# Linear attention and a gated feed-forward on one core: gates of two more token chunks by seven products, elementwise work moved to GpSimd, and a new order of steps

## The chip, the core and the metric

The kernel runs on one core of a Trainium2 chip. A core has TensorE (PE, with its weight loads shown as PEld), VectorE (DVE), ScalarE (ACT), GpSimd (POOL) and SyncE (SP). Each engine works through its own queue in order and waits there on semaphores, and DMAs are issued from the queues of SP, POOL and ACT. The metric is device time in microseconds (us): the time before is the median of three runs.

## What is computed

```python
def phi(x): return where(x > 0, x, exp(x) - 1) + 1          # = min(exp(x), max(x, 0) + 1)
q_p, k_p = phi(q), phi(k)                                    # q, k, v: 8 batches, 8 heads, 576 rows, 64
kv  = einsum('bhsd,bhse->bhde', k_p, v);  z = sum(k_p, axis=2)
num = einsum('bhsd,bhde->bhse', q_p, kv)
x   = num / (einsum('bhsd,bhd->bhs', q_p, z)[..., None] + 1e-6)   # as 4608 rows of 512
out = ((x @ w1) * (x @ w2)) @ w3 @ w_out                     # w1, w2: 512x1024, w3: 1024x1024, w_out: 1024x512
```

All inputs and the output are f32 in memory. On the chip the products take bf16 and add up in f32.

## The kernel before

The 4608 rows are cut into nine chunks of 512. Chunks 0 to 7 hold the first 512 rows of a batch each, and chunk 8 the last 64 rows of all eight. w3 and w_out are first multiplied to one matrix, `wf_sb` (1024x512), so that a chunk needs its gate, (x w1)(x w2), a tile `ab` of 1024x512 in bf16, and then one product with `wf_sb`.

The whole program is one list of steps, the string `ORDER`, from which `step` calls one small function for each word. The list fixes the order on every engine: each engine does its own instructions in the order in which the steps stand. A trailing "+" chooses the second engine for the elementwise part of a step (for a load: the POOL queue instead of SP's). The letters that matter here, with batch or chunk b:

- `Lb.g`, `Mb.g`, `Nb.g`: loads of half a batch of k, q, v (512 KB) into a tile of the pool `ld`, which has 13 buffers. `Rb.0`, `Rb.1`: the last 64 rows of q and k, and of v.
- `xb.g` and `Xb.g` (k and q): `phi_exp`, exp on ACT. `yb.g`, `Yb.g`: `phi_max1`, max(x, 0) + 1, of f32 to bf16. `zb.g`, `Zb.g`: `phi_min`, the minimum of the two, bf16. A half of 128x1024 is done in two instructions of 128x512. g = 2 stands for the last rows, of q and k together.
- `vb.g`: v to bf16. `Kb`: `kv_full`, the 18 matmuls of kv and z of a batch and the copy out of PSUM. `Tb.0`: a DMA transpose of phi(q).
- `Ab.j`: `nat`, four matmuls for 128 rows of num and den, then three DVE instructions (add 1e-6, reciprocal, product) that write x (`xn`). `Db.0`: a DMA transpose of the chunk's x into `xt`, on SP's queue; `Db.1` for the last rows.
- `Fb.f`: `f_unit`, one of eight gate tiles of a chunk with eight matmuls: four give x w1 (`a_ps`), four x w2 (`b_ps`), each of 128x512; ACT copies the one to SBUF, DVE multiplies it with the other.
- `Gb.q.i`: `g_unit`, product i (1 to 7) of quarter q. Four quarters of seven products (Winograd's form of Strassen's scheme) give a chunk's gate: each product is four matmuls of 128x256 with weights out of w1, w2 or their sums (`ws_make`, steps `e`), and with columns of x or of their differences (`xs_make`, steps `db.i`). Products 1, 3 and 4 are copied to SBUF by ACT, products 2, 5 and 6 are added to such a copy by DVE, product 7 is copied in half by ACT and multiplied by DVE.
- `mb.q.i`: `g_mul`, the f32 product (128x256) that makes a block of `ab` from the sums of products 2, 5 and 6.
- `Ob.m`: `o_unit`, eight matmuls of 128x512 with `wf_sb` and a copy. `S`, `H`, `Q`: stores of the output.

Before the change, chunks 0 to 5 take the eight tiles of `F`, and chunks 6, 8 and 7 (in this order) the 28 products of `G`. The sums of weights and of x, and the ring of twelve f32 tiles for `G`, are laid into buffers of `ld` that no load needs any more (`from_ld`); `f_close` has a ring of four f32 tiles of its own. All `e`, `d`, `m` and `y` steps run on DVE. PSUM has four buffers for `mm` (`a_ps`, `b_ps` and the products `t`, `t2`), and three single ones, of which `ou0`/`ou1` hold `u` of the products or the sums of `O`.

Of the kernel before, what the change touches and what calls it, by code (L numbers as in the profile page):

```python
# [20 lines left out]
def kernel(  # L21
# [177 lines left out]
    def phi_min(name, b, g):
# [7 lines left out]
        e, y = (t.rearrange("p (c u j d) -> p c u j d", c=2, u=2, d=D) for t in (e, y))  # L207
        for c in range(2):
            nc.vector.tensor_tensor(out=p[0][:, 2 * g + c].rearrange("p j u d -> p u j d"),  # L209
                                    in0=e[:, c], in1=y[:, c], op=ALU.min)  # L210
# [519 lines left out]
```

## Time and profile before

| | |
|---|---|
| median of three runs | 250.21 us (249.04 to 250.46) |
| the profiled execution | 249.9 us, of which 248.0 us are the span from its first to its last instruction |
| granted TensorE clock, mean | 0.991 |
| ACT busy | 131.9 us (53%) |
| DMA | 49.43 MB, 199 GB/s over the span |

A "line" such as L422 is a line of the program. A group of the profile reads: line, engine, operation, out<-in, shape, xcount | busy us, mean ns of one | idle time before it and what ended it. A window reads: its length, then busy us and number of instructions for PE, PEld, DVE, ACT and POOL, the granted clock, the busy share of the DMA engines (which may pass 1, as packets of several queues overlap), and GB/s. A piece of the chain of waits reads: its start, its length, what ran. The releasers are inferred from semaphores.

### The profile page before, as it was taken

The page shows a single profiled execution, that of the slowest core. Times are in us where ns is not written, and L with a number is a line of the kernel's source. Part 1 is how long each engine was busy: PE and PEld are TensorE (multiplying, and loading weights), DVE is VectorE, ACT ScalarE, POOL GpSimd, SP SyncE. Part 2 cuts the span into 40 slices and gives each one's busy share as a digit, 9 for nine tenths or more (in the row PEclk, how much of TensorE's full clock was granted, in tenths as well). Part 3 has the DMA queues.
Part 4 walks back from the last instruction along what each step waited for, and adds up shares of the span by engine and source line. Part 5 has one row for each costly group of instructions (what it writes and reads, how often), then busy time and mean ns, then how long its engine had stood idle before and what let it go on. Part 6 is the DMA issues. An engine that isn't in the chain of part 4 may idle for free.

```text
span 248.0 us, 4281 instructions
## 1 busy us (share of the span) xinstructions
PE 230.9 (93%) x1548; PEld 133.6 (54%) x1548; DVE 187.4 (76%) x434; ACT 131.9 (53%) x213; POOL 49.4 (20%) x79
## 2 busy tenths in 40 slices
PE   0699868999999999999999999999999999999994
PEld 0445455654454554345445544545488688578542
DVE  3227769777898847788768799988899999779810
ACT  2206667658756725675563383536466377245321
POOL 8546368665014050500000000000000000000000
PEclk9999988999999999999999999999999999999999
DMA  7999999999999999999999999917750133040144
GB/s 159 193 202 310 295 211 211 194 259 288 287 219 329 236 234 273 217 304 282 288 362 268 284 270 221 295 37 174 169 193 0 22 65 107 3 169 1 44 152 145
DMA packets 64021, 49.43 MB, mean 199 GB/s; under 512 B 32480, under 2 KB 58848, under 8 KB 64000
## 3 DMA queue, kind: packets, MB, share of 16 engines
q1 hardware_dynamic: 52928, 36.31, 58.3%
q0 software_dynamic: 10928, 12.72, 25.2%
q8 instruction: 12, 0.20, 0.3%
q10 hardware_dynamic: 144, 0.13, 0.2%
q14 instruction: 9, 0.07, 0.1%
HBM read 38.80 MB, written 9.44 MB: 194 GB/s over the span
## 4 chain that ended last, share of the span: by engine, by line
PE 67%; DMA 21%; ACT 3%; DVE 3%; SPq 2%; issue 2%; POOL 0%; ACTq 0%; DVEq 0%; POOLq 0%
PE o_ps L536 21%; PE a_ps L362 12%; PE b_ps L362 12%; DMA q<-in_q_dram 10%; PE gu L422 9%; DMA w3b<-in_moe_w_dram 7%; PE gt L422 6%; DMA k<-in_k_dram 4%; PE nd L310 3%; PE kvp L245 2%; SPq L104 1%; ACT e L179 1%; PE o_ps L561 1%; PE kvp L249 1%; DVE qj L209 1%
## 5 line engine op out<-in xcount | busy, mean ns | idle before, releaser
L536 PE MATMUL o_ps<-wf_sb,ab 128*128 128x512 bf16 x280 | 64.2, 379 | 0.0
L362 PEld LDWEIGHTS <-w_sb 128*128 128x128 bf16 x384 | 36.5, 98 | 40.6 <-issue 0.8
L362 PE MATMUL a_ps<-xt,w_sb 128*128 128x512 bf16 x192 | 50.3, 379 | 0.5 <-ACT a_sb L367 0.5
L362 PE MATMUL b_ps<-xt,w_sb 128*128 128x512 bf16 x192 | 50.3, 379 | 0.0
L536 PEld LDWEIGHTS <-ab 128*128 128x128 bf16 x280 | 26.8, 98 | 29.3
L368 DVE TENSOR_TENSOR ab<-a_sb,b_ps 128x512 bf16<-128x512 f32 x48 | 32.5, 683 | 11.5 <-PE b_ps L362 5.9
L538 ACT COPY o_sb<-o_ps 128x512 f32<-128x512 f32 x30 | 17.4, 585 | 42.8 <-PE o_ps L536 28.8
L367 ACT COPY a_sb<-a_ps 128x512 f32<-128x512 f32 x48 | 27.7, 585 | 22.2 <-PE a_ps L362 21.8
L326 DVE TENSOR_TENSOR xn<-nd,r 128x512 bf16<-128x512 f32 x30 | 20.7, 691 | 1.0
L422 PEld LDWEIGHTS <-spare 128*128 128x128 bf16 x192 | 18.7, 98 | 2.2
L179 ACT ACTIVATE e<-q 128x1024 bf16<-128x1024 f32 x16 | 16.8, 1057 | 5.7 <-DMA q<-in_q_dram 5.0
L310 PE MATMUL nd<-kv,qt 128*128 128x130 bf16 (+1 forms) x160 | 16.6, 228 | 2.9 <-ACT kv L254 1.8
L179 ACT ACTIVATE e<-k 128x1024 bf16<-128x1024 f32 x16 | 16.8, 1056 | 3.2 <-DMA k<-in_k_dram 3.1
L310 PEld LDWEIGHTS <-qt 128*128 128x128 bf16 (+1 forms) x160 | 11.8, 103 | 12.2 <-issue 3.5
L454 DVE TENSOR_TENSOR spare<-spare,gt 128x512 f32<-128x512 f32 x24 | 16.1, 680 | 1.8 <-PE gt L422 0.9
L154 PE MATMUL wf_ps<-wt_sb,w3t 128*128 128x512 bf16 x64 | 16.5, 403 | 0.6 <-DMA wt_sb<-in_moe_w_out_dram 0.6
L450 ACT COPY spare<-gu 128x512 f32<-128x512 f32 x24 | 13.6, 587 | 3.9 <-PE gu L422 3.7
L422 PEld LDWEIGHTS <-w_sb 128*128 128x128 bf16 x144 | 14.0, 98 | 2.7 <-issue 0.3
L465 DVE TENSOR_TENSOR ab<-spare 128x256 bf16<-128x256 f32 x36 | 14.1, 417 | 0.1
L114 POOL DMA_DIRECT2D qk32r<-in_q_dram x14 | 9.0, 644 | 23.3 <-ACT a_sb L367 10.7
L209 DVE TENSOR_TENSOR qj<-e,y 128x512 bf16<-128x512 bf16 x32 | 12.1, 418 | 2.0 <-ACT e L179 1.8
L422 PE MATMUL gu<-spare 128*128 128x256 bf16 x96 | 13.4, 272 | 0.0
(87 smaller groups left out, 294.0 us busy)
## 6 DMA issues: line engine op xcount, KB each, us to landing
out_dram<-o_sb SPq DMA_DIRECT2D x15, 512.0 KB, 3.9
q<-in_q_dram SPq DMA_DIRECT2D x13, 512.0 KB, 8.1
k<-in_k_dram SPq DMA_DIRECT2D x12, 512.0 KB, 7.0
v<-in_v_dram SPq DMA_DIRECT2D x12, 512.0 KB, 9.0
w3b<-in_moe_w_dram POOLq DMA_DIRECT2D x8, 256.0 KB, 10.0
...
```

What stands on the lines that cost most here:

```text
L154: nc.tensor.matmul(wfs[i], w3ts[i][:, kc, :], wo_sb[:, kc, :], start=(kc == 0), stop=(kc == FC - 1))
L179: nc.scalar.activation(out=e, in_=x, func=AF.Exp)
L209: nc.vector.tensor_tensor(out=p[0][:, 2 * g + c].rearrange("p j u d -> p u j d"), in0=e[:, c], in1=y[:, c], op=ALU.min)
L310: nc.tensor.matmul(nds[g][rows, i * 2 * E1:(i + 1) * 2 * E1], w, kvs[b % 2][:, i, g].rearrange("p u e -> p (u e)"), start=True, stop=True)
L326: nc.vector.tensor_tensor(out=dst.rearrange("p (g h) e -> p g h e", g=2), in0=v4[:, :, :, 0:D], in1=r[rows].unsqueeze(3).to_broadcast([n, ...
L362: nc.tensor.matmul(ps, w[:, kc, f * P:(f + 1) * P], xt_of(c)[:, :, kc, :], start=(kc == 0), stop=(kc == KC - 1))
L367: nc.scalar.copy(out=a_sb, in_=a_ps)
L368: nc.vector.tensor_mul(out=abs_[c][:, f, :], in0=a_sb, in1=b_ps)
L422: nc.tensor.matmul(t[:, w], l, r, start=(first and w == 0 and k == 0), stop=(k == 1), skip_group_check=True)
L454: nc.vector.tensor_tensor(out=s, in0=o, in1=t, op=ALU.add)
L536: nc.tensor.matmul(o_ps, ab[:, f, m * P:(m + 1) * P], wf_sb[:, f, :], start=(f == 0), stop=(f == FC - 1))
L538: copy_of(alt)(out=rows_of(c, m // 2)[:, m % 2], in_=o_ps)
```

## The change

- Chunks 4 and 5 are also done by seven products. Now 56 products of `G` and 24 `m` steps take the place of 16 `F` steps, and eight `d` steps come with them.
- The sums of weights go into `wo_sb` (w_out's own tile, free after `wf_sb` is made, and no longer shared with another) and the new `wx_sb`; the differences of x go into a pool of two tiles `xs`. The f32 tiles of `G` and `F` share one ring of eight. The pool `ld` shrinks from 13 buffers to 8.
- A half's minimum of phi is one instruction of 128x1024 rather than two of 128x512, for which phi(k), phi(q) and the transposed phi(q) are laid out by j and then c.
- On GpSimd now: all eight `e` steps, eight of the 32 maxima of a half and one of the last rows, 11 of the 20 `d` steps and 43 of the 60 `m` steps. Eight `O` copies rather than five are on DVE.
- From the step behind `L4.0` on, the list of steps is in a new order. The part before that is unchanged. Functions that no step called are removed.

```diff
-    ld = ctx.enter_context(tc.tile_pool(name="ld", bufs=13))
+    ld = ctx.enter_context(tc.tile_pool(name="ld", bufs=8))
...
-    wt_sb = wpool.tile([P, 4, FC // 2, HN], BF16)
-    wo_sb = wt_sb.rearrange("p i (a c) n -> p (i a) (c n)", c=2)
+    wo_sb = wpool.tile([P, FC, DM], BF16)
+    wx_sb = wpool.tile([P, 4, 2, NQ * P], BF16)
...
-            p[0] = t[:, 0:JW].rearrange("p (c j u d) -> p c j u d", j=NJ, u=2, d=D)
+            p[0] = t[:, 0:JW].rearrange("p (j c u d) -> p c j u d", j=NJ, u=2, d=D)
+            p[2] = t[:, 0:JW].rearrange("p (j h d) -> p h j d", j=NJ, d=D)
...
-        e, y = (t.rearrange("p (c u j d) -> p c u j d", c=2, u=2, d=D) for t in (e, y))
-        for c in range(2):
-            nc.vector.tensor_tensor(out=p[0][:, 2 * g + c].rearrange("p j u d -> p u j d"),
-                                    in0=e[:, c], in1=y[:, c], op=ALU.min)
+        e, y = (t.rearrange("p (h j d) -> p h j d", j=NJ, d=D) for t in (e, y))
+        nc.vector.tensor_tensor(out=p[2][:, 4 * g:4 * g + 4], in0=e, in1=y, op=ALU.min)
...
-            qts[b, 0] = t[:, 0:NB].rearrange("p (c j) t -> p c (j t)", j=NJ)
+            qts[b, 0] = t[:, 0:NB].rearrange("p (j c) t -> p j c t", j=NJ)
...
-        a_sb = sm.tile([P, NCH], F32, tag="f", name="a_sb", bufs=4)
+        a_sb = fsm("a_sb").rearrange("p a n -> p (a n)")
...
-        s[i] = from_ld(("w", w, i // 2), [P, 2, 2, NQ * P], BF16)[:, i % 2]
+        s[i] = wx_sb[:, i] if w else wo_sb.rearrange("p (i k) n -> p i k n", k=2)[:, i]
...
-            xss[c] = from_ld(("x", c), [P, 4, 2, 2, P], BF16)
+            xss[c] = xt_p.tile([P, 4, 2, 2, P], BF16, tag="xs", name="xs", bufs=2)
...
     def fsm(name):
-        if not spare.get("ring"):
-            spare["ring"] = True
-            for n in range(6):
-                t = from_ld(("f", n), [P, 2, 2, HN], F32)
-                ring.extend((t[:, 0], t[:, 1]))
-        return ring.pop(0)
+        return sm.tile([P, 2, HN], F32, tag="f", name=name, bufs=8)
...
-    v3.1 S0.1 A2.1 y3.1 R5.1+ z3.0 z3.1 v3.0 v3.2 O1.1+ O1.0 T3.0 D2.0 S0.0 L4.0 K3 R4.1+ R4.0+ O1.3
-    A3.0 O1.2 A3.2 L4.1 v4.2+ F2.6 A3.3 F2.3 N4.1 y4.0 F2.1 M4.0 x4.0 A3.1 x4.1 F2.0 M4.1 y4.2 v5.2+
...
-    G7.3.2 G7.1.2 G7.3.7 m7.3.2 m7.3.6 m7.1.2 O8.2 m7.3.5 O8.3 m7.0.5 O7.0 m7.2.6 O7.1 H8.2 m7.2.5
-    H8.3 O8.0 m7.1.6 S7.0 O8.1+ S8.0 O7.2 H7.2 Q7.3
+    v3.1 S0.1 A2.1 y3.1 R5.1+ z3.0 z3.1 v3.0 v3.2 O1.1+ O1.0 T3.0 D2.0 S0.0 L4.0 R4.0+ L4.1 x5.2
+    M4.0 y4.2 x4.2 M4.1 R4.1+ R6.0+ z5.2 y4.0+ K3+ N4.0 O1.2 v5.2+ A3.0 z4.2 v4.2+ F2.6 A2.4 F2.7
+    M5.1 N4.1 F2.0 y6.2 A3.3 x4.1 x4.0 z4.0 M5.0 F2.2 y4.1+ F2.4 M6.0 e1.0+ S1.0 z4.1 X4.0 v4.0+
+    Y4.0 X4.1 X5.1 O1.3 A3.2 Y4.1+ e1.2+ Z4.1 Y5.1 R7.0+ v4.1 F2.3 F2.1 K4 F2.5 e0.2+ S1.1 A3.1 Z5.1
+    x6.2 R6.1+ X5.0 O2.0+ X6.0 Z4.0 O2.3 Y5.0 Z5.0 L5.0 x5.0 O2.2 x7.2 Y6.0 y5.0 D3.0 v6.2 A3.4 T4.0
+    z5.0 O2.1 L5.1 F3.0 F3.7 Z6.0 y7.2+ e1.1+ A4.2 x5.1 z6.2 F3.5 M6.1 M7.0 y5.1 F3.2 A4.0 X6.1 z5.1
+    F3.3 N5.1 N5.0 L6.0 X7.0 N6.0 L6.1 e0.0+ S2.0 v5.0+ v5.1 F3.1 Y6.1+ x6.0 A4.1 S2.1 F3.6 F3.4
+    y6.0+ T5.0 A4.3 Z6.1 O3.3+ x6.1 v6.0 K5 O3.2 O3.1 y6.1 z6.0 D4.0 D1.1 e1.3+ z6.1 Y7.0 N6.1 Z7.0
+    z7.2 N7.1 A5.3 e0.1+ O3.0 e0.3+ d4.0 d4.2 d4.1+ A5.2 G4.1.1 G4.1.2 G4.0.1 L7.1 G4.0.4 A5.0
+    m4.1.2+ v6.1+ G4.1.3 G4.1.4 G4.0.3 G4.1.5 G4.0.6 d4.3+ G4.2.4 G4.0.5 G4.1.7 v7.1 G4.0.2 A5.1
+    R7.1+ m4.1.5+ m4.0.6+ L7.0 G4.0.7 G4.3.1 G4.3.4 m4.0.5+ y7.1+ G4.3.2 S3.0 x7.0 G4.3.3 G4.1.6
+    G4.2.1 m4.1.6+ A4.4 D5.0 m4.0.2+ G4.2.2 G4.3.5 G4.3.6 G4.2.3 d5.0 m4.3.2+ T6.0 K6 G4.2.5 G4.3.7
+    v7.2 G5.3.4 m4.2.2+ M7.1 m4.3.6+ A5.4 G4.2.7 y7.0+ G5.0.4 G4.2.6 x7.1 G5.1.4 A6.3 O4.1 S3.1 d5.2
+    m4.3.5+ z7.1 X7.1 m4.2.5+ m4.2.6+ N7.0 d5.1+ z7.0 A6.0 O4.2+ Y7.1+ D3.1 Z7.1 O4.3 T7.0 A6.4
+    G5.0.1 G5.1.1 G5.1.2 G5.0.3 v7.0 d5.3+ A6.2 G5.1.3 S4.1 G5.0.6 G5.0.5 m5.1.2+ G5.0.2 K7 G5.1.5
+    G5.0.7 G5.1.6 A6.1 m5.0.2+ m5.0.6+ G5.1.7 O4.0 m5.1.5+ D6.0 m5.0.5+ A7.4 G5.3.1 G5.3.2 G5.2.1
+    m5.1.6+ m5.3.2 G5.2.2 m5.2.2+ G5.3.3 G5.3.6 G5.2.4 d6.0 m5.3.6+ G5.2.3 G5.3.5 d6.1+ G5.2.6
+    G6.0.4 G5.2.5 G5.3.7 m5.2.6+ A7.2 G6.1.4 G5.2.7 m5.3.5+ d6.3 d6.2+ G6.1.1 G6.3.4 G6.1.2 G6.1.3
+    D5.1 D7.1 A7.0 G6.0.1 G6.1.5 S4.0 m5.2.5+ m6.1.2+ G6.1.6 G6.0.3 G6.0.6 m6.1.6+ G6.1.7 G6.0.5
+    m6.0.5+ A7.1 d8.0 d8.1+ G6.0.2 O5.1 d8.3+ G6.0.7 m6.0.2 G6.2.4 G6.3.1 m6.1.5 A7.3 D7.0 m6.0.6+
+    O5.0 G6.3.3 G6.3.6 G6.2.1 G6.3.2 G6.3.5 G6.2.3 d8.2+ m6.3.2+ G8.1.4 G6.2.6 G6.2.5 G6.3.7 m6.3.6+
+    S5.0 m6.2.6 G6.2.2 m6.3.5 G8.0.4 G6.2.7 O5.3 m6.2.2+ m6.2.5+ O5.2 G8.1.1 d7.0 d7.2 G8.1.2 G8.0.1
+    m8.1.2+ G8.0.2 G8.1.3 d7.1+ G8.0.3 m8.0.2 d7.3+ G8.1.6 G7.1.4 G8.0.5 G8.1.5 m8.0.5 G8.2.4
+    m8.1.6+ G8.0.7 G8.3.4 G8.1.7 G8.0.6 m8.1.5+ m8.0.6 O6.2 G8.3.1 G8.3.2 G8.2.1 G8.3.3 m8.3.2 S5.1
+    G8.3.6 G8.2.3 G8.3.5 G8.2.2 G8.2.5 G8.3.7 G8.2.6 G7.0.4 m8.2.5 G8.2.7 m8.2.2+ m8.3.6+ m8.3.5
+    O6.3+ m8.2.6+ O6.0+ O6.1 G7.0.1 G7.0.2 G7.1.1 G7.0.3 S6.1 G7.0.6 G7.1.3 S6.0 G7.0.5 G7.2.4
+    m7.0.5 G7.1.5 G7.0.7 G7.1.6 G7.1.2 m7.1.6+ G7.1.7 O8.2+ O8.3 G7.2.1 m7.1.5 G7.2.2 m7.0.2+ G7.3.1
+    m7.1.2 G7.2.3 G7.3.2 G7.3.3 G7.2.5 m7.2.2+ G7.3.4 m7.2.5 G7.3.5 G7.2.7 G7.2.6 G7.3.6 G7.3.7 H8.3
+    O8.0+ H8.2 m7.3.5+ O8.1 m7.3.2+ O7.0 S8.0 m7.2.6 O7.1 m7.3.6 m7.0.6+ O7.2 S7.0 H7.2 Q7.3
```

107 lines of the change are left out of this document (9 added, 98 removed).

## The prediction

> **What bounds the kernel now.** I read the page's busy times and slices first, then the chain of waits, then three stretches of the span.
>
> ```profile
> span 248.0 us, 4281 instructions
> PE 230.9 (93%) x1548; PEld 133.6 (54%) x1548; DVE 187.4 (76%) x434; ACT 131.9 (53%) x213; POOL 49.4 (20%) x79
> PE   0699868999999999999999999999999999999994
> DVE  3227769777898847788768799988899999779810
> PE 67%; DMA 21%; ACT 3%; DVE 3%; SPq 2%; issue 2%; POOL 0%; ACTq 0%; DVEq 0%; POOLq 0%
> PE o_ps L536 21%; PE a_ps L362 12%; PE b_ps L362 12%; DMA q<-in_q_dram 10%; PE gu L422 9%; DMA w3b<-in_moe_w_dram 7%; PE gt L422 6%; DMA k<-in_k_dram 4%; PE nd L310 3%; PE kvp L245 2%; SPq L104 1%; ACT e L179 1%; PE o_ps L561 1%; PE kvp L249 1%; DVE qj L209 1%
> 50.00:174.00 124.00, 122.80 (x721) 61.12 (x720) 101.80 (x234) 71.58 (x110) 19.05 (x31) 1.00 1.04 256
> 174.00:236.00 62.00, 61.99 (x481) 45.16 (x480) 54.74 (x125) 32.47 (x63) 0.00 (x0) 1.00 0.27 78
> ```
>
> TensorE is busy without a break from about 50 us to 236 us. Busy can mean waiting, so I compared the pace of the two ways to make a gate with each other, in pieces of the chain:
>
> ```profile
> 64.68 0.86 PE a_ps L362 x4
> 65.54 0.86 PE b_ps L362 x4
> 186.42 0.87 PE gt L422 x8
> 187.30 0.87 PE gu L422 x8
> ...
> L422 PEld LDWEIGHTS <-spare 128*128 128x128 bf16 x192 | 18.7, 98 | 2.2
> ```
>
> Four matmuls of 512 columns take 0.86 us, and eight of 256 take 0.87 us: in both cases the time goes with the columns, and the extra weight loads of the products, 98 ns each at a pace of 109, are hidden. So TensorE is the bound, and only fewer columns or fewer of the remaining gaps shorten the run. VectorE is second: 54.74 of 62 us in the last stretch, where the products run, and GpSimd did nothing there at all. That is why the products were not free to spread: they need more elementwise work.
>
> **What TensorE saves.** An F step is 0.86 + 0.86 = 1.72 us; 16 of them are 27.5 us. A product is half of 0.87, and 56 of them are 24.4 us. The difference is **-3.2 us**, if nothing else comes to bound.
>
> **What VectorE and ScalarE pay.**
>
> ```profile
> L368 DVE TENSOR_TENSOR ab<-a_sb,b_ps 128x512 bf16<-128x512 f32 x48 | 32.5, 683 | 11.5 <-PE b_ps L362 5.9 <-ACT a_sb L367 5.1 <-PE tpr L277 0.2
> L454 DVE TENSOR_TENSOR spare<-spare,gt 128x512 f32<-128x512 f32 x24 | 16.1, 680 | 1.8 <-PE gt L422 0.9 <-ACT spare L450 0.7
> L459 DVE TENSOR_TENSOR ab<-spare,gu 128x256 bf16<-128x256 f32 x12 | 4.9, 416 | 0.6 <-ACT spare L458 0.6
> L465 DVE TENSOR_TENSOR ab<-spare 128x256 bf16<-128x256 f32 x36 | 14.1, 417 | 0.1
> L209 DVE TENSOR_TENSOR qj<-e,y 128x512 bf16<-128x512 bf16 x32 | 12.1, 418 | 2.0 <-ACT e L179 1.8
> L184 DVE TENSOR_SCALAR y<-k 128x1024 bf16<-128x1024 f32 x16 | 11.1, 692 | 2.7 <-DMA k<-in_k_dram 2.7
> L396 DVE TENSOR_TENSOR spare<-w_sb 128x1024 bf16<-128x1024 bf16 x4 | 2.7, 685 | 0.0
> L407 DVE TENSOR_TENSOR spare<-xt 128x512 bf16<-128x512 bf16 x4 | 1.7, 419 | 0.6 <-DMA xt<-xn 0.6
> L538 DVE COPY o_sb<-o_ps 128x512 f32<-128x512 f32 x5 | 3.4, 687 | 8.4 <-PE o_ps L536 8.3
> L367 ACT COPY a_sb<-a_ps 128x512 f32<-128x512 f32 x48 | 27.7, 585 | 22.2 <-PE a_ps L362 21.8
> L450 ACT COPY spare<-gu 128x512 f32<-128x512 f32 x24 | 13.6, 587 | 3.9 <-PE gu L422 3.7
> L458 ACT COPY spare<-gu 128x256 f32<-128x256 f32 x12 | 4.5, 373 | 4.9 <-PE gu L422 4.2 <-DVE ab L459 0.5
> ```
>
> VectorE: 16 gate products go (-10.9), 24 sums of 0.680 and 8 products of 0.416 come (+19.6). It does 17 `m` steps rather than 36 (-7.9), 9 `d` steps rather than 12 (-1.3), no `e` step (8 x 0.685, -5.5), and eight maxima fewer (-5.5). A minimum of 128x1024 in one piece should cost what the bf16 instruction of that size at L396 does, 0.685 rather than 2 x 0.418: 32 times -0.15 are -4.8. Three copies of `o_ps` more are +2.1. Sum: about -14 of 187 us. ScalarE: -16 x 0.585, + 24 x 0.587 + 8 x 0.373, - 3 x 0.585: +6, to some 138 us. Both stay far under TensorE over the whole.
>
> **What GpSimd pays.** No row shows an elementwise product on it, so its price is bounded by what it has done:
>
> ```profile
> L714 POOL MEMSET const-float32-0.0<- 128x1 f32 x1 | 0.1, 98 | 0.2 <-issue 0.2
> masks.py:197 POOL MEMSET ident<- 128x128 bf16 x1 | 0.3, 272 | 0.0
> masks.py:199 POOL TENSOR_SCALAR_AFFINE_SELECT ident<-ident 128x128 bf16<-128x128 bf16 x1 | 0.3, 287 | 0.1
> L114 POOL DMA_DIRECT2D v32r<-in_v_dram x14 | 8.7, 627 | 14.0 <-DVE vr L221 10.7 <-DMA v32r<-in_v_dram 1.3 <-DMA qk32r<-in_k_dram 1.1
> ```
>
> From 1 to 128 elements the memset grows by 1.37 ns an element; one input (287) adds nearly nothing. I take 98 ns + 1.37 ns an element with one input and twice the slope with two: an `m` step 0.80, a `d` step 1.50, an `e` step 2.90, a maximum of a half 1.50. The low end is VectorE's own rows (0.417, 0.42, 0.685, 0.69). The high end is 287 ns for 128 elements without a fixed part, doubled for two inputs: 1.15, 2.30, 4.60, 2.30.
>
> The densest stretch of the new order runs from `O3.2` (just behind `K5`) to `G6.1.7`. It holds 68 products, 7 `O`, 14 `A` and 2 `K` on TensorE, and on GpSimd 25 `m`, 6 `d`, 3 `e`, 3 maxima and two loads of v's last rows.
>
> ```profile
> L310 PE MATMUL nd<-kv,qt 128*128 128x130 bf16 (+1 forms) x160 | 16.6, 228 | 2.9 <-ACT kv L254 1.8
> L245 PE MATMUL kvp<-vt,kj 128*128 128x130 bf16 x96 | 7.1, 219 | 0.0
> L249 PE MATMUL kvp<-vr,qj 128*128 128x260 bf16 x16 | 4.4, 273 | 0.0
> L324 DVE TENSOR_SCALAR r<-nd 128x8 f32<-128x8 f32 x30 | 4.8, 160 | 6.2 <-PE nd L310 6.0
> L325 DVE RECIPROCAL r<-r 128x8 f32<-128x8 f32 x30 | 6.1, 203 | 1.1
> L326 DVE TENSOR_TENSOR xn<-nd,r 128x512 bf16<-128x512 f32 x30 | 20.7, 691 | 1.0
> ```
>
> TensorE: 68 x 0.435 + 7 x 1.72 + 14 x 0.42 (16.6 / 40) + 2 x 1.73 (7.1 / 6 + 4.4 / 8) = 51 us. VectorE: 28 sums, 9 gate products, 14 times 1.05 for `A`, 6 minima, 2 maxima, 6 `d`, and three smaller steps make about 47. GpSimd: 25 x 0.80 + 6 x 1.50 + 3 x 2.90 + 3 x 1.50 + 2 x 0.63 = 43.5 us; 18 at the low end, 64.5 at the high one. At my price it fits behind TensorE's 51 with a sixth to spare, so I charge nothing for it; at the high end it would be late by 13.
>
> The Trainium skill, in the GPSIMD Engine Reference, section 3.1 (Elementwise), puts a two-input operation at about 2.6 cycles of 1.2 GHz an element, and in section 4.1 (Engine selection) advises against GpSimd for elementwise products as it is about twice as slow as VectorE. By that an `m` step is an estimated 0.55 us and the stretch some 31, which would leave the sum as it is; no row here shows it.
>
> **New waits, +1.1 us.** First, `D5.0` now stands close in front of its use. From `A5.1`, its last input, to `G5.3.4`, the first product that reads a difference of chunk 5, TensorE has 13 products, one `A` of half the rows and `K6`, 5.7 + 0.2 + 1.7 = 7.6 us. Against it stand 1.05 us for `A` on VectorE, 0.42 for `d5.0`, and the transpose:
>
> ```profile
> DMA to landing us min/median/max: 2.5/4.8/8.9
> ```
>
> (the DMA transposes of L351). With the median that is 6.3 us and fits, with the longest 10.4 and is 2.8 late; VectorE waits at `d5.0` with the sum of `G4.2.5` and the half-product of `G4.3.7` behind it, and TensorE stops when their banks are not emptied. I charge 0.5 (0 to 2.8). Second, `Z7.1` stands two short VectorE steps behind its maximum `Y7.1`, which queues on GpSimd behind three `m` and `d5.1`: 0.2 (0 to 1). Third, VectorE and GpSimd may slow each other down (below): 0.4 (0 up to the rival's price).
>
> **A small gain at the start, -0.3 us.** The order there is the same, but the chain holds 1% of `qj` minima (2.5 us), which get 18% shorter: 0 to -0.45. The other edits cost nothing by themselves: with eight load buffers rather than 13 a load waits for the eighth before it, which by the order has long been read (`L7.1` is the tightest, about ten us of TensorE ahead of its use); the ring of eight f32 tiles leaves at the least one product's time, 0.44 us, between the release of a tile and the next writer. That cover is thin: a late `m` on GpSimd would show as ScalarE waiting, then TensorE.
>
> **Sum:** 249.9 (span 248.0 + 1.9 around it) - 3.2 - 0.3 + 1.1 = 247.5 for an execution like the profiled one, which lies 0.3 under the median; so 247.8 against 250.2, 1% faster.
>
> **Rivals.** (A) *GpSimd becomes the bound of the dense stretch.* It takes in-order work there that everything waits for: `d` steps before products, `m` steps that give back f32 tiles and, at the end of a chunk, hold up `O`. It decides from 1.18 times my price (51 / 43.5). At 1.35 times it is 58.7, 7.5 late; 249.9 + 7.5 - 3.2 = 254; at the high end, 260. For it: no spare tile, and a price without a row. Against: the memsets. The same end is reached by contention: VectorE's instructions with two inputs in SBUF, or copies from it at double rate, take in that stretch 6 minima, 6 `d`, 1 `m` and 2 maxima, about 8.5 us; if they doubled while GpSimd works, VectorE would need 55.5 rather than 47, 4.5 over TensorE: 251. The Trainium skill says in the GPSIMD Engine Reference, sections 1 (Specifications) and 8 (Key points), that GpSimd shares its SBUF interfaces with VectorE and contends with just such instructions; no run so far shows it.
>
> (B) *The loads bind.* Counted in TensorE's time of the steps in front, the new order wants the first half of q of batch 6 some 20 us earlier and that of batch 7 some 30 us earlier on ScalarE's queue, which also empties PSUM, and the DMA engines are at 1.04 of their time from 50 to 174 us. Each load that lands late stops both. Against it: their tiles are free ten us or more ahead. Two late landings of 1.5 us each would cost what was saved: 250.
>
> (C) *The sum is right and the waits don't come*, since VectorE is relieved: 249.9 - 3.2 - 0.5 = 246.2.
>
> (D) *The products don't save.* If the weight loads were late behind other traffic, 56 products could take the 27.5 us of what they replace: 250. The pace of 0.87 speaks against it.
>
> **How the numbers follow.** My forecast 0.50, A 0.26, B 0.10, C 0.12, D 0.02. A measurement tells about 0.5%, 1.25 us, from no change. C and nine tenths of the forecast lie under 248.96: faster 0.57. D, half of B and what is left of the forecast are within: 0.13 with a little of A; A for the most part and half of B make slower 0.30. The range goes from just under C, 245.8, to A at 1.35 times, 254; the forecast's own is 246 to 249.
>
> **What would show it.** Right: 224 more matmuls of 128x256 at 0.435 a product; minima of 128x1024 near 0.685; GpSimd under 90 us busy behind the loads; VectorE near 173 us; no new gap of TensorE over half a us from `G4` on but at `d5.0`. Wrong: `m` steps over 0.94 us on GpSimd, VectorE's two-input instructions longer than before, ScalarE waiting on GpSimd for its f32 tile, or on a load of q.

## The result, and the profile after

| | before | after |
|---|---|---|
| median | 249.62 us (248.40 to 250.46, 4 runs) | 273.13 us (271.21 to 273.99, 4 runs) |
| ratio to before, 95% interval | | 1.0935 (1.0857 to 1.1013) |
| span of the profiled execution | 248.0 us | 269.2 us |

The kernel became 9% slower; the prediction had been 1% faster, with a range that ended at 254 us. The page of the changed kernel answers to the one shown of before as follows (busy times and share of the span, the slices, the chain that ended last).

```profile
span 269.2 us, 4565 instructions
PE 236.9 (88%) x1644; PEld 143.8 (53%) x1644; DVE 198.0 (74%) x377; ACT 138.6 (51%) x231; POOL 144.5 (54%) x150
...
PE   0699969999999995698989499986989999999994
...
DVE  3237897778888768999879959859888867747720
...
POOL 8445596573202399991549359993484727202310
...
PE 29%; POOL 7%; DVE 3%; DMA 2%; ACT 1%; issue 0%; POOLq 0%; DVEq 0%
```

Three things are to be seen. TensorE has lost its unbroken row of nines between the 16th and the 30th slice (about 101 to 202 us). GpSimd's own nines stand in the same part, from the 15th to the 27th slice, but for one in the 6th. And VectorE, which was to lose 14 us of work, has gained 11 (187.4 to 198.0) with 57 instructions fewer. The groups, with different shapes kept apart, say which instructions grew:

```profile
L440 POOL TENSOR_TENSOR ab<-gc 128x256 bf16<-128x256 f32 x43 | 32.6, 777 | 43.5 <-DVE gc L431 39.9 <-DVE r L315 3.4
...
L201 DVE TENSOR_TENSOR qj<-e,y 128x1024 bf16<-128x1024 bf16 x16 | 20.6, 1290 | 5.1 <-POOL y L176 4.0 <-ACT e L171 0.7
L176 POOL TENSOR_SCALAR y<-k 128x1024 bf16<-128x1024 f32 x5 | 18.4, 3677 | 8.2 <-DVE xnr L317 4.6 <-DVE r L316 3.5
...
L201 DVE TENSOR_TENSOR kj<-e,y 128x1024 bf16<-128x1024 bf16 x16 | 15.7, 995 | 2.0 <-ACT e L171 1.1 <-POOL y L176 0.9
...
L176 POOL TENSOR_SCALAR y<-q 128x1024 bf16<-128x1024 f32 x3 | 11.2, 3749 | 9.9 <-DMA q<-in_q_dram 9.3 <-DVE kj L201 0.6
L391 POOL TENSOR_TENSOR xs<-xt,xs 128x512 bf16<-128x512 bf16 x7 | 8.9, 1270 | 5.2 <-DVE xs L391 5.2
...
L380 POOL TENSOR_TENSOR wo_sb<-w_sb 128x1024 bf16<-128x1024 bf16 x2 | 4.7, 2350 | 0.0
L380 POOL TENSOR_TENSOR wx_sb<-w_sb 128x1024 bf16<-128x1024 bf16 x2 | 4.2, 2112 | 0.0
```

On GpSimd the f32 products `m` take 777 ns, the differences `d` 1270, the sums of weights `e` 2.1 to 2.4 us (rows for four of the eight), and a maximum 3.7 us. On VectorE the minima, meant to take 0.685 us, take 1.29 and 0.995 in the mean. Their work is the same each time, and the fastest take 0.68, so something beside them makes the others long. The next view is the timeline of the worst place, first VectorE and then GpSimd (start, length, instruction, idle time before it; the last three lines of each are from 142 us on):

```profile
100.60 2.60 DVE L201 TENSOR_TENSOR kj<-e,y 128x1024 bf16<-128x1024 bf16 x1 [0.88 <-POOL y L176]
...
103.73 1.52 DVE L176 TENSOR_SCALAR y<-q 128x1024 bf16<-128x1024 f32 x1
...
107.33 2.60 DVE L201 TENSOR_TENSOR qj<-e,y 128x1024 bf16<-128x1024 bf16 x1 [1.04 <-POOL y L176]
...
112.38 1.87 DVE L359 TENSOR_TENSOR ab<-a_sb,b_ps 128x512 bf16<-128x512 f32 x3
...
115.21 0.68 DVE L201 TENSOR_TENSOR qj<-e,y 128x1024 bf16<-128x1024 bf16 x1
...
116.79 5.61 DVE L201 TENSOR_TENSOR qj<-e,y 128x1024 bf16<-128x1024 bf16 x1
...
142.04 2.55 DVE L201 TENSOR_TENSOR qj<-e,y 128x1024 bf16<-128x1024 bf16 x1
...
145.11 2.01 DVE L176 TENSOR_SCALAR y<-k 128x1024 bf16<-128x1024 f32 x1
147.04 3.21 DVE L201 TENSOR_TENSOR kj<-e,y 128x1024 bf16<-128x1024 bf16 x2
```

```profile
100.55 2.11 POOL L380 TENSOR_TENSOR wx_sb<-w_sb 128x1024 bf16<-128x1024 bf16 x1
103.30 4.00 POOL L176 TENSOR_SCALAR y<-q 128x1024 bf16<-128x1024 f32 x1 [0.64 <-DVE kj L201]
107.27 2.11 POOL L380 TENSOR_TENSOR wx_sb<-w_sb 128x1024 bf16<-128x1024 bf16 x1
...
111.85 2.59 POOL L380 TENSOR_TENSOR wo_sb<-w_sb 128x1024 bf16<-128x1024 bf16 x1
...
115.64 2.03 POOL L176 TENSOR_SCALAR yr<-qk32r 128x512 bf16<-128x512 f32 x1
117.66 2.11 POOL L380 TENSOR_TENSOR wx_sb<-wx_sb,w_sb 128x1024 bf16<-128x1024 bf16 x1
119.74 2.11 POOL L380 TENSOR_TENSOR wo_sb<-w_sb 128x1024 bf16<-128x1024 bf16 x1
...
141.91 2.13 POOL L380 TENSOR_TENSOR wx_sb<-w_sb,wx_sb 128x1024 bf16<-128x1024 bf16 x1
144.00 2.57 POOL L380 TENSOR_TENSOR wo_sb<-wo_sb,w_sb 128x1024 bf16<-128x1024 bf16 x1
146.65 2.45 POOL L380 TENSOR_TENSOR wo_sb<-w_sb,wo_sb 128x1024 bf16<-128x1024 bf16 x1
```

A weight sum starts on GpSimd at 100.55 and ends at 102.66; the minimum that starts at 100.60 on VectorE ends at 103.20, half a us behind it. The same happens at 107.3. At 116.8 a minimum begins beside the end of a maximum of the last rows, isn't done when that ends at 117.67, and then outlasts two sums, until 122.4. In all five places where a minimum met a sum, it ends 0.54 to 0.56 us behind the end of a sum. In between, three gate products `ab` (112.38), which have one of their inputs in PSUM, run beside a sum and take 1.87 us together, their usual pace. So VectorE's minimum is held until GpSimd's two-input instruction is done, and does most of its own work behind it; and as VectorE works in order, the steps that TensorE needs next stand behind the minimum. TensorE's waits from 93 to 200 us name them (engine and line, what it waited for, us in total, times, longest):

```profile
PE nd L301 <- DVE xn L317: 4.0, 1, 4.0
PE kvp L236 <- DVE xn L317: 3.1, 1, 3.1
PE o_ps L455 <- DVE ab L359: 3.0, 2, 2.2
PE nd L301 <- DVE xnr L317: 2.4, 1, 2.4
```

All four are VectorE's small in-order work, late. The longest shows it best:

```profile
153.07 0.62 PE L301 MATMUL nd<-kv,qt 128*128 128x130 bf16 x4 [3.99 <-DVE xn L317]
```

TensorE stands still from 149.1 to 153.1 us for an `xn` that VectorE could start only at 152.3. Ahead of it in VectorE's queue stood a minimum, a maximum and a minimum (142.04, 145.11 and 147.04) that ran beside three sums and took 5 us more than they take alone.

A gap can also cost afterwards. Three times in this trace the granted clock falls to half, 3.0 to 4.5 us after the start of a gap of TensorE (those from 103.2, 111.5 and 149.1 us). The windows inside these stretches read (length, PE, PEld, DVE, ACT, POOL, granted clock, DMA share, GB/s):

```profile
107.70:111.00 3.30, 3.30 (x11) 1.35 (x10) 3.27 (x2) 2.49 (x5) 3.30 (x4) 0.50 0.49 167
114.50:117.90 3.40, 3.40 (x10) 1.18 (x8) 3.07 (x5) 0.00 (x0) 3.38 (x4) 0.50 0.57 124
152.10:158.80 6.70, 5.73 (x31) 4.34 (x32) 4.46 (x12) 2.13 (x4) 3.80 (x5) 0.50 0.73 247
```

Half of TensorE's busy time there, (3.30 + 3.40 + 5.73) / 2 = 6.2 us, is an estimate of what this cost on top of the idle time. From 118 to 152 us and from 159 to 204 us the clock is 1.00, although a gap of 2.4 us lies in the latter, at 182 us; so not every gap is followed by a slow stretch, and what decides it is not shown.

To keep a ledger I counted, by the trace, what each stretch of the span holds beyond the time of its columns at the pace of 0.86 us for 2048. The columns alone are 218.9 us before and 215.5 after: the saving of 3.4 is there. What lies beyond them (the two last kernels are experiments that follow):

| us beyond the columns | before | after | sums on VectorE | sums, maxima, differences on VectorE |
|---|---|---|---|---|
| up to 100 us | 21.0 | 20.5 | 22.0 | 22.0 |
| from there to the end of `K5` (before: to 140) | 2.1 | 12.7 | 4.4 | 6.3 |
| from there to `G6.1.7` (before: to 200) | 1.4 | 14.8 | 11.2 | 6.3 |
| the rest | 4.6 | 5.7 | 5.4 | 5.9 |
| sum | 29.1 | 53.7 | 43.0 | 40.5 |

Of the loss of 24.6 us, 24.0 lie between 100 and 205 us.

### The profile page after: what moved, and what is told of

Read it like the earlier page. It is cut to its first block, busy times and chain, and to the rows that moved or that the text cites. A ratio compares the mean times of both kernels' runs of the same rounds, so it can differ in the third digit from the quotient of the medians.

```text
span 269.2 us, 4565 instructions
## 1 busy us (share of the span) xinstructions
PE 236.9 (88%) x1644; PEld 143.8 (53%) x1644; DVE 198.0 (74%) x377; ACT 138.6 (51%) x231; POOL 144.5 (54%) x150
## 5 line engine op out<-in xcount | busy, mean ns | idle before, releaser
L440 POOL TENSOR_TENSOR ab<-gc 128x256 bf16<-128x256 f32 x43 | 32.6, 777 | 43.5 <-DVE gc L431 39.9
L353 PE MATMUL b_ps<-xt,w_sb 128*128 128x512 bf16 x128 | 35.5, 394 | 0.4 <-DVE ab L359 0.4
L353 PE MATMUL a_ps<-xt,w_sb 128*128 128x512 bf16 x128 | 35.4, 393 | 0.0
L431 DVE TENSOR_TENSOR gc<-gs,gt 128x512 f32<-128x512 f32 x40 | 27.0, 683 | 10.4 <-ACT gs L427 9.0
L427 ACT COPY gs<-gu 128x512 f32<-128x512 f32 x40 | 22.8, 588 | 17.0 <-PE gu L406 14.1
L359 DVE TENSOR_TENSOR ab<-a_sb,b_ps 128x512 bf16<-128x512 f32 x32 | 21.3, 683 | 9.5 <-PE b_ps L353 4.9
L201 DVE TENSOR_TENSOR qj<-e,y 128x1024 bf16<-128x1024 bf16 x16 | 20.6, 1290 | 5.1 <-POOL y L176 4.0
L358 ACT COPY a_sb<-a_ps 128x512 f32<-128x512 f32 x32 | 18.1, 585 | 10.3 <-PE a_ps L353 10.2
L176 POOL TENSOR_SCALAR y<-k 128x1024 bf16<-128x1024 f32 x5 | 18.4, 3677 | 8.2 <-DVE xnr L317 4.6
L406 PEld LDWEIGHTS <-wo_sb 128*128 128x128 bf16 x160 | 15.5, 100 | 5.0 <-issue 1.2
L201 DVE TENSOR_TENSOR kj<-e,y 128x1024 bf16<-128x1024 bf16 x16 | 15.7, 995 | 2.0 <-ACT e L171 1.1
```

What stands on the lines that cost most here:

```text
L176: (nc.gpsimd if alt else nc.vector).tensor_scalar(out=y, in0=x, scalar1=0.0, scalar2=1.0, op0=ALU.max, op1=ALU.add)
L201: nc.vector.tensor_tensor(out=p[2][:, 4 * g:4 * g + 4], in0=e, in1=y, op=ALU.min)
L353: nc.tensor.matmul(ps, w[:, kc, f * P:(f + 1) * P], xt_of(c)[:, :, kc, :], start=(kc == 0), stop=(kc == KC - 1))
L359: nc.vector.tensor_mul(out=abs_[c][:, f, :], in0=a_sb, in1=b_ps)
L406: nc.tensor.matmul(t[:, w], l, r, start=(first and w == 0 and k == 0), stop=(k == 1), skip_group_check=True)
L427: nc.scalar.copy(out=s, in_=t)
```

## The experiments

Each experiment gives its time as a ratio to the kernel before on the same chip, since chips differ by some tenths of a us.

### Parts of GpSimd's work put back on VectorE

Four kernels take a trailing "+" away and leave everything else: the eight sums of weights (e_dve), the nine maxima (y_dve), both (ye_dve), or all that is elementwise on GpSimd (all_dve). For the sums:

```diff
-    M5.1 N4.1 F2.0 y6.2 A3.3 x4.1 x4.0 z4.0 M5.0 F2.2 y4.1+ F2.4 M6.0 e1.0+ S1.0 z4.1 X4.0 v4.0+
+    M5.1 N4.1 F2.0 y6.2 A3.3 x4.1 x4.0 z4.0 M5.0 F2.2 y4.1+ F2.4 M6.0 e1.0 S1.0 z4.1 X4.0 v4.0+
...
-    z7.2 N7.1 A5.3 e0.1+ O3.0 e0.3+ d4.0 d4.2 d4.1+ A5.2 G4.1.1 G4.1.2 G4.0.1 L7.1 G4.0.4 A5.0
+    z7.2 N7.1 A5.3 e0.1 O3.0 e0.3 d4.0 d4.2 d4.1+ A5.2 G4.1.1 G4.1.2 G4.0.1 L7.1 G4.0.4 A5.0
```

> The changed kernel with its eight weight sums back on VectorE (0.685 each, 5.5 us in all), the maxima left on GpSimd. Price theory: 268 to 273, as GpSimd's queue is only 18 us of its 145 shorter. Hold theory: minima and maxima on VectorE at their own 0.69 again, 14 us of waiting gone: 256 to 262.

> The changed kernel with its nine maxima of phi back on VectorE, in the same places of the order. Price theory (the maxima at 3.7 us on GpSimd, 0.69 on VectorE, are what holds up the minima, kv and the rest): most of the 23 us come back, 250 to 256. Hold theory (VectorE's two-input instructions wait while a two-input instruction of GpSimd runs, at the weight sums above all): only a few us come back, 264 to 270, and minima of 2.6 us are still seen. If both matter in equal parts: 257 to 263.

> Both back on VectorE; GpSimd keeps 43 f32 products (0.73) and 11 differences of x (1.16). Both theories: what is left is TensorE's saving of 3.2 us against short waits: 246 to 250. If the differences and products hold VectorE as well: 251 to 255.

> Nothing elementwise on GpSimd: 43 products (0.417) and 11 differences (0.42) come to VectorE too. In the stretch from O3.2 to G6.1.7 VectorE then needs some 64 us against 51 of TensorE, so 13 us are late if that stretch is bound by it: 256 to 262. If the move of these two to GpSimd was of no use: the same as with maxima and sums alone on VectorE.

| | median | ratio to before |
|---|---|---|
| after | 273.13 us | 1.0935 (1.0857 to 1.1013) |
| e_dve | 260.50 | 1.0418 (1.0351 to 1.0484) |
| y_dve | 269.17 | 1.0765 (1.0687 to 1.0843) |
| ye_dve | 263.74 | 1.0545 (1.0474 to 1.0616) |
| all_dve | 269.00 | 1.0753 (1.0659 to 1.0846) |

Eight sums of weights, which cost VectorE 5.5 us, give back 12.6 us when it does them. With them gone from GpSimd the minima are nearly what they should be, though the maxima are still on GpSimd (groups of e_dve):

```profile
L201 DVE TENSOR_TENSOR qj<-e,y 128x1024 bf16<-128x1024 bf16 x16 | 12.2, 760 | 3.6 <-POOL y L176 2.3 <-ACT e L171 1.0
L201 DVE TENSOR_TENSOR kj<-e,y 128x1024 bf16<-128x1024 bf16 x16 | 10.8, 684 | 1.7 <-ACT e L171 1.4 <-POOL y L176 0.3
```

The 32 minima fall from 36.3 to 23.0 us. Part of the gain is the clock: in e_dve it falls to half only once in this part, in a window from 172.7 to 176.0 us with 3.30 us of TensorE, or 1.7 us lost by the same estimate rather than 6.2. ye_dve was expected below e_dve and lies above it. The reason is in its waits: VectorE itself now waits in front of a maximum for its load of k.

```profile
DVE y L176 <- DMA k<-in_k_dram: 9.0, 2, 8.2
```

`y4.0+` stands early in the list, right behind its load. As a step of VectorE it blocks that queue for 8.2 us. So these two runs say nothing of the price of the maxima, and the step had to be moved.

### The same with the first maximum moved behind its load

`y4.0` now stands in front of `z4.0`. y2_dve has the nine maxima on VectorE, ye2_dve the sums too, yed2_dve also the eleven differences (GpSimd keeps 43 `m`), all2_dve everything.

```diff
-    M4.0 y4.2 x4.2 M4.1 R4.1+ R6.0+ z5.2 y4.0+ K3+ N4.0 O1.2 v5.2+ A3.0 z4.2 v4.2+ F2.6 A2.4 F2.7
-    M5.1 N4.1 F2.0 y6.2 A3.3 x4.1 x4.0 z4.0 M5.0 F2.2 y4.1+ F2.4 M6.0 e1.0+ S1.0 z4.1 X4.0 v4.0+
+    M4.0 y4.2 x4.2 M4.1 R4.1+ R6.0+ z5.2 K3+ N4.0 O1.2 v5.2+ A3.0 z4.2 v4.2+ F2.6 A2.4 F2.7
+    M5.1 N4.1 F2.0 y6.2 A3.3 x4.1 x4.0 y4.0 z4.0 M5.0 F2.2 y4.1 F2.4 M6.0 e1.0+ S1.0 z4.1 X4.0 v4.0+
```

> As the run with the nine maxima back on VectorE, but y4.0 stands right in front of z4.0, where its load of k has landed, rather than ten steps ahead, where VectorE waited 8 us for that load. Load theory (that wait was an artefact of the place): 8 to 9 us less than 269, 259 to 262; the holds by the weight sums stay. If the wait only moves: 266 to 270.

> Maxima and weight sums on VectorE, y4.0 moved as well. Load theory: 8 to 9 us less than 263.7, so 254 to 256; if the two moves together undo all that the change cost, 246 to 250.

> The 11 differences of x on VectorE as well; GpSimd keeps only the 43 f32 products. Hold theory: the differences (1.16 to 1.26 us on GpSimd) delay the products that read them and hold minima, differences and products of VectorE: 2 to 4 us better than with them on GpSimd, 250 to 253. If VectorE is the bound of the product stages by now: the same or up to 2 us worse.

> Nothing elementwise on GpSimd, y4.0 moved. VectorE would need some 64 us for the stretch from O3.2 to G6.1.7 against 51 of TensorE: 257 to 262. If it comes to the same as with the 43 products on GpSimd, their move was worth nothing.

| | on GpSimd | median | ratio to before |
|---|---|---|---|
| y2_dve | 8 sums, 11 differences, 43 products | 265.69 us | 1.0592 (1.0523 to 1.0661) |
| ye2_dve | 11 differences, 43 products | 260.57 | 1.0409 (1.0353 to 1.0464) |
| yed2_dve | 43 products | 258.14 | 1.0324 (1.0265 to 1.0382) |
| all2_dve | none | 267.86 | 1.0656 (1.0575 to 1.0736) |

All four are 4 to 6 us above the first range that was expected of them: the move of `y4.0` gave back 3 to 4 us rather than the 8 of its wait, and with it the loss was not undone. The prices of the parts don't add up either. The maxima are worth 8.6 us while the sums are beside them on GpSimd (1.0935 to 1.0592, times 250) and nothing once the sums are gone (1.0418 to 1.0409). Sums and maxima together are worth 13. The eleven differences are worth 2, with intervals that overlap. The products are the one part that pays: back on VectorE they cost 8 us. With only those on GpSimd the minima stand at 687 and 686 ns.

### Hold, or lateness?

Taking the sums off GpSimd removes two things: the hold on VectorE, and 18 us of GpSimd's queue with the sums' own lateness. e_dummy leaves the sums on VectorE as in e_dve and puts, in their places on GpSimd, sixteen additions into a tile that nobody reads. They can be late for no one, except for what is queued behind them on GpSimd.

```diff
-        (nc.gpsimd if alt else nc.vector).tensor_tensor(out=s[i], in0=a(), in1=b(), op=op)
+        nc.vector.tensor_tensor(out=s[i], in0=a(), in1=b(), op=op)
+        for n in range(2):
+            nc.gpsimd.tensor_tensor(out=scratch, in0=t[:, n, 0:NCH], in1=t[:, 2 + n, 0:NCH], op=op)
```

> The changed kernel with its weight sums on VectorE, as e_dve (260.5), and in their places on GpSimd two additions of 128x512 in bf16 each, with two inputs, into a tile that nobody reads: GpSimd is as busy as in the changed kernel, but nobody waits for a result. Hold theory (VectorE's two-input instructions and GpSimd's own queue are held up while such an addition runs): most of the 12.6 us are there again, 268 to 275, and minima of 1.2 to 2.5 us are seen. If it was the lateness of the sums themselves: 260 to 263.

It took 270.01 us, 1.0778 (1.0713 to 1.0843): 9 of e_dve's gain are gone again. Its groups:

```profile
L383 POOL TENSOR_TENSOR scratch<-w_sb 128x512 bf16<-128x512 bf16 x16 | 21.7, 1358 | 0.9
...
L202 DVE TENSOR_TENSOR qj<-e,y 128x1024 bf16<-128x1024 bf16 x16 | 14.9, 931 | 3.6 <-POOL y L177 2.3 <-ACT e L172 1.0
L202 DVE TENSOR_TENSOR kj<-e,y 128x1024 bf16<-128x1024 bf16 x16 | 13.6, 862 | 0.5 <-ACT e L172 0.4
```

The additions hold GpSimd for 21.7 us rather than the 18.1 of the sums, in shorter pieces; the minima grow by 5.5 us rather than by 13.3. So this run shows that work on GpSimd that nobody waits for costs 9 of the 12.6 us. The clock has a share in it here too: windows of e_dummy at 0.50 hold 5.50, 3.30 and 3.30 us of TensorE, an estimated 6.1 us lost rather than the 1.7 of e_dve. The run does not part the hold on VectorE from the delay of what is queued on GpSimd behind the additions, the maxima above all.

### The old order, and the ring of eight

old_order is the changed code with the order of before and nothing elementwise on GpSimd, chunks 4 and 5 by `F`. In it the `m` steps of the last chunks had to move forward so that eight f32 tiles suffice. old_m puts 20 of its 36 `m` on GpSimd; old_r12 has the exact order of before, a ring of twelve and, to make room for it, six load buffers.

```diff
-    ld = ctx.enter_context(tc.tile_pool(name="ld", bufs=8))
+    ld = ctx.enter_context(tc.tile_pool(name="ld", bufs=6))
...
-        return sm.tile([P, 2, HN], F32, tag="f", name=name, bufs=8)
+        return sm.tile([P, 2, HN], F32, tag="f", name=name, bufs=12)
...
-    G8.1.5 G8.3.4 m6.3.2 G8.1.6 m8.0.2 G8.0.7 G8.1.7 G8.2.4 D7.0 G8.1.2 m8.0.5 d7.0 G8.2.1 S5.1 G8.3.1 m8.1.5
+    G8.3.4 G8.1.6 m8.0.2 G8.0.7 G8.1.7 G8.2.4 m6.1.5 D7.0 G8.1.2 m8.0.5 d7.0 G8.2.1 S5.1 G8.3.1 G8.0.6 G8.2.3
```

> The changed kernel's code (long minima, own tiles for the sums, eight load buffers, one ring of eight) with the list of steps of the kernel before: six tiles of F for chunk 0 and eight for chunks 1 to 5, nothing elementwise on GpSimd; six f32 products stand up to 18 steps earlier, as the ring is shorter. If the new tiles and buffers cost nothing and the minima save their 0.15 us each: 248 to 250. If eight load buffers or the ring of eight are what binds: 253 or more.

> As old_order, with 20 of the 36 f32 products of chunks 6, 8 and 7 on GpSimd, the same ones as in the changed kernel. VectorE's 14.1 us of products shrink by 8.3 in the stretch where it is at 88%. If a product on GpSimd costs 0.73 and holds little: 0 to 2 us less than old_order. If it holds VectorE's two-input work: the same or slower.

> The kernel old_order (258) with a ring of twelve f32 tiles and six load buffers instead of eight and eight, and every step exactly where the kernel before has it. Ring theory (the products of the old order hold up to 11 tiles at once; with eight, ScalarE's copies wait for VectorE and TensorE for both, 9 us of gaps from 186 us on): 248 to 251. Load theory (fewer buffers for loads are what costs): 258 or more.

| | median | ratio to before |
|---|---|---|
| old_order | 258.05 us | 1.0310 (1.0257 to 1.0362) |
| old_m | 253.98 | 1.0160 (1.0111 to 1.0209) |
| old_r12 | 252.75 | 1.0095 (1.0060 to 1.0130) |

The smaller ring with the order it forces costs 5.4 us (1.0310 to 1.0095), and the waits show it at its place. From 150 us on, ScalarE of old_order waits for VectorE to give f32 tiles back; in old_r12 the same line has one such wait.

```profile
ACT gs L427 <- DVE gc L431: 10.2, 12, 1.6
...
ACT ga L434 <- DVE gc L431: 7.9, 5, 2.2
```

```profile
ACT gs L427 <- DVE gc L431: 1.2, 1, 1.2
```

20 products on GpSimd give 4 of these us back (old_m): the two waits fall from 18.1 to 7.6 us, as VectorE gets sooner to the sums that release tiles. What old_r12 still loses against the kernel before, 2.4 us and clear of its interval, was not taken apart; it has, among other things, six load buffers rather than 13 and tiles of its own for the sums.

old_g45 adds the seven products for chunks 4 and 5 to old_m, in blocks of two quarters at the places of the `F` steps, with sums and differences on VectorE.

```diff
-    Y6.0 F4.5 y6.1 F4.7 v6.0+ x6.1 L7.0 x6.0 M7.0 A5.3 D3.1 x7.0 z6.1 F4.0 v6.1+ v6.2 F4.6 A4.4 Z6.0
+    Y6.1 Z6.1 A5.0 Y6.0 d4.0 d4.1 d4.2 d4.3 G4.0.1 G4.1.1 G4.0.2 m4.0.2+ G4.1.2 m4.1.2+ G4.0.4 G4.1.4
+    G4.0.3 G4.1.3 G4.0.6 m4.0.6+ G4.1.6 m4.1.6+ G4.0.5 m4.0.5+ G4.1.5 m4.1.5+ G4.0.7 G4.1.7 y6.1 v6.0+ x6.1 L7.0
```

> As old_m, with chunks 4 and 5 by seven products too, in blocks of two quarters at the places where their F steps stood, weight sums and differences on VectorE and spread ahead, the products on GpSimd that are there in the changed kernel. If seven products for two more chunks are sound and the new order was at fault: 246 to 250. If VectorE and the waits of the products eat TensorE's 3.2 us in any order: 251 to 256.

It took 276.20 us, 1.1043 (1.0982 to 1.1105). From 120 to 200 us TensorE waits for VectorE for 17.4 us in all. Products in such blocks cost 22 us (1.0160 to 1.1043), so this run is no test of the idea in itself; whether they would have saved anything if spread over the order of before was not tried.

### The ring in the new order

yed2_r10 is yed2_dve with ten f32 tiles and seven load buffers.

```diff
-    ld = ctx.enter_context(tc.tile_pool(name="ld", bufs=8))
+    ld = ctx.enter_context(tc.tile_pool(name="ld", bufs=7))
...
-        return sm.tile([P, 2, HN], F32, tag="f", name=name, bufs=8)
+        return sm.tile([P, 2, HN], F32, tag="f", name=name, bufs=10)
```

> The 258 us version with a ring of ten f32 tiles and seven load buffers. If the ring of eight binds in the new order too (gaps of 6 us in the product stages from 136 to 198 us beyond those of before): 254 to 256.5. The new order was laid out for eight, so if the gaps come from sums, differences and transposes that are late: 257 to 259.

259.90 us, 1.0384 (1.0348 to 1.0420), against 1.0324 (1.0265 to 1.0382) with eight: nothing gained. The new order is laid out for eight. One load buffer fewer came with the longer ring, and the run doesn't part the two.

### The stretch from 100 to 140 us

In yed2_dve, TensorE still loses 6.3 us there, and the waits from 80 to 200 us name steps of batch 4 and their neighbours:

```profile
PE kvp L236 <- DVE xn L317: 3.1, 2, 2.5
PE kvp L236 <- ACT vt L206: 1.3, 1, 1.3
```

Two attempts: the loads of batch 4 further ahead in SP's queue (yed2_ld), or its phi and kv later in the list (yed2_late). For the first:

```diff
-    v3.1 S0.1 A2.1 y3.1 R5.1+ z3.0 z3.1 v3.0 v3.2 O1.1+ O1.0 T3.0 D2.0 S0.0 L4.0 R4.0+ L4.1 x5.2
-    M4.0 y4.2 x4.2 M4.1 R4.1+ R6.0+ z5.2 K3+ N4.0 O1.2 v5.2+ A3.0 z4.2 v4.2+ F2.6 A2.4 F2.7
+    v3.2 O1.1+ O1.0 L4.0 L4.1 T3.0 D2.0 M4.0 M4.1 N4.0 S0.0 R4.0+ x5.2 y4.2 x4.2 R4.1+
+    R6.0+ z5.2 K3+ O1.2 v5.2+ A3.0 z4.2 v4.2+ F2.6 A2.4 F2.7 M5.1 N4.1 F2.0 y6.2 A3.3
```

> The 258 us version (maxima, weight sums and differences on VectorE) with the loads of batch 4 two or five transposes and a store earlier in SP's queue (two ahead of T3.0, three behind D2.0). Load theory (phi of batch 4 is wanted 12 to 17 us after the transposes and waits for its loads, 5 us of TensorE between 99 and 112 us): 253 to 256. If the wait lies elsewhere: 257 to 260.

> The 258 us version (maxima, weight sums and differences on VectorE) with phi and kv of batches 4 and later moved back by some 4 to 6 us of TensorE's time, so that F2 and O steps stand in front of them while the loads of batch 4 land. If the new order calls for batch 4 before its loads are there (gaps of 5 us between 87 and 112): 253 to 256. If the work is only late elsewhere then: 257 to 261.

Both were slower than yed2_dve: 265.19 us, 1.0626 (1.0554 to 1.0698), and 263.95 us, 1.0525 (1.0476 to 1.0575). In yed2_ld the store `S0.0` now stands in SP's queue behind five loads, and ScalarE, which needs the tile of the output back, stands still:

```profile
ACT o_sb L457 <- DMA out_dram<-o_sb: 14.8, 1, 14.8
```

In yed2_late the waits move: from 80 to 200 us TensorE waits 3.9 us for gate products of `F` and 3.2 for differences of x.

### The long minima by themselves

b_longmin is the kernel before with the minima in one piece; b_longmin_m also puts 20 of its 36 `m` on GpSimd (ring of twelve, order of before).

```diff
-        e, y = (t.rearrange("p (c u j d) -> p c u j d", c=2, u=2, d=D) for t in (e, y))
-        for c in range(2):
-            nc.vector.tensor_tensor(out=p[0][:, 2 * g + c].rearrange("p j u d -> p u j d"),
-                                    in0=e[:, c], in1=y[:, c], op=ALU.min)
+        e, y = (t.rearrange("p (h j d) -> p h j d", j=NJ, d=D) for t in (e, y))
+        nc.vector.tensor_tensor(out=p[2][:, 4 * g:4 * g + 4], in0=e, in1=y, op=ALU.min)
```

> The kernel before with nothing changed but the minima of phi, in one instruction of 128x1024 with the layout by j. If they save what was worked out (4.8 us of VectorE over the run, 0.3 us at the start on the chain): 249 to 250.3. If the layout costs elsewhere (kv, transposes): 251 or more.

> The kernel before with the long minima and with 20 of its 36 f32 products on GpSimd, the same ones as there in the changed kernel; 13 load buffers and the ring of twelve tiles as before. VectorE is relieved by 8.3 us where it is at 88%, and the tiles are long enough. If GpSimd's products (0.73) come in time: 247.5 to 249.5, better than before. If TensorE was not held up by VectorE there anyway: 249.5 to 250.5. If they are late for O or for a tile: 251 or more.

249.83 us, 1.0001 (0.9969 to 1.0033), and 251.15 us, 1.0020 (0.9983 to 1.0057). The minima take 0.685 and 0.687 us as predicted, and the time stays: VectorE is not what the kernel before waits for. With 20 `m` on GpSimd the 16 that stay on VectorE take 549 ns rather than 417, so 2.1 of the 8.3 us that were moved come back, and again the time doesn't follow. No version tried was faster than the kernel before.

## Why the prediction was wrong

**What bounds the kernel, and what TensorE saves (-3.2): right.** The columns fell by 3.4 us, and in the last stretch, where no sum of weights and no maximum runs on GpSimd, the products keep their pace (5.7 us beyond the columns, before 4.6).

**VectorE -14: right in the instructions, wrong in their durations.** 187.4 became 198.0 us, 25 more than the predicted 173. Of these, 14 are the minima (36.3 us rather than 32 x 0.685), and nearly 5 the 24 maxima left on VectorE (21.3 us by the groups of after rather than 24 x 0.69). One of them took 2.0 us beside a sum, two 1.0 and 1.5 beside a maximum, and one 2.5, most of it beside four DMA issues of GpSimd. The other 6 are a slip of the sum: I took whole durations off a busy time in which neighbouring instructions overlap, by 20.3 us in all before and by 14.6 after. ScalarE's +6 was right (131.9 to 138.6).

**What GpSimd pays.** The prices by kind:

| | predicted | measured, mean |
|---|---|---|
| `m` | 0.80 us (0.42 to 1.15) | 0.78 |
| `d` | 1.50 (0.42 to 2.30) | 1.25 (13.7 us for 11) |
| `e` | 2.90 (0.69 to 4.60) | 2.26 (18.1 us for 8) |
| maximum of a half | 1.50 (0.69 to 2.30) | 3.70 (29.6 us for 8) |

The two-input prices were 3 to 28% too high. The maximum lies beyond the high end: I had taken one input to mean the slope of a memset. The Trainium skill, in the GPSIMD Engine Reference, section 4.1 (Engine selection), says that one-input operations run roughly at line rate there; the trace disagrees, with 3.6 us at the least for 1024 elements of f32 to bf16, against 0.69 on VectorE and 2.1 for a two-input sum of the same size in bf16 on GpSimd.

**The step that failed is "At my price it fits behind TensorE's 51 with a sixth to spare, so I charge nothing for it", with its companion, the third new wait ("VectorE and GpSimd may slow each other down (below): 0.4").** The window of after for just that stretch, from the end of `K5` to `G6.1.7`, reads:

```profile
143.30:204.90 61.60, 52.51 (x426) 38.67 (x424) 51.02 (x98) 31.10 (x59) 43.51 (x39) 0.94 0.64 149
```

GpSimd is busy for 43.51 us, which is what was priced, by luck: sums and differences were cheaper and maxima dearer. TensorE is busy for 52.5. Still the stretch takes 61.6. No engine's sum binds; each waits for another in turn. TensorE waits 4.0 us behind the three sums at 142 to 149 us, 2.4 for an `xnr` behind a minimum that first waited 2.9 for a maximum on GpSimd and then ran for 1.64 beside a difference, 1.0 for a product on GpSimd and 0.8 for a difference, and by the estimate above 2.9 go to the clock. Comparing sums of busy time over 50 us was the wrong test: three queues in order, each of which hands the next its input, don't overlap just because each sum fits. With GpSimd's sums, maxima and differences back on VectorE the same stretch takes 52.9 us.

And I looked only at that stretch. Of the 24.6 us that the ledger has lost (29.1 to 53.7), 10.6 came before it, between 100 and 143 us, where I hadn't priced GpSimd's sums and maxima at all, and where the minima stand that are held. Rival A named the mechanism, but let two-input instructions double, and put it in the dense stretch, at 251 us. Of the five minima that met a sum four went from 0.69 to 2.6 us and one to 5.6. (In its sums, 51 / 43.5 is 1.17 and 58.7 - 51 is 7.7, rather than 1.18 and 7.5; nothing hangs on it.) The Trainium skill has the rule that gives this size, in SBUF — State Buffer, section "SBUF: two separate sides": VectorE and GpSimd share one pair of ports as an exclusive lock held for a whole instruction, so the loser blocks fully. The trace agrees for sums against minima (2.11 us of a sum, 2.60 for the minimum beside it); for a maximum on GpSimd against a minimum it agrees only in part: the three minima that ran beside a maximum in e_dve took 0.68 to 0.91 us, but the one of 116.79 in after was not done 0.87 us after it began beside one.

What the experiments settle: the weight sums on GpSimd cost 12.6 us, the maxima 8.6 beside them and nothing without them (13 together), the differences about 2; the products gain 8. What they leave open is how the cost of the sums divides into hold and queue. The clock's share of it is estimated at 4.5 us (6.2 in after, 1.7 in e_dve), from one profiled execution of each.

**New waits.** The transpose `D5.0`, charged 0.5, left TensorE no wait over 0.8 us for a difference of x. The maxima that VectorE waits for, charged 0.2, cost its minima 4.9 us of idle time.

**The start, -0.3, and the long minima:** their duration came as predicted, and no time with it (b_longmin).

**"The other edits cost nothing by themselves":** wrong for the ring of eight in the order of before (5.4 us), as "That cover is thin" had hinted, but in the new order ten tiles gain nothing. The load buffers were not tested alone, and 2.4 us between old_r12 and the kernel before are unexplained.

**What stays open.** yed2_dve, with only the products on GpSimd, is still 8 us slower than before although its columns are 3.4 us shorter. The ledger puts 4 us of it between 100 and 139 us and 5 in the dense stretch. Rival B, the loads, may have a part in the first (ScalarE waits in all 9.9 us for loads of k, 3.5 at the longest; in the kernel before 3.1 and 1.8), but the two attempts on it made things worse. Whether another order could bring out the saving was not shown.
